# A fold of two weight matrices: w3 turned by VectorE in 32x32 squares instead of transposed on TensorE

## The chip, the cores and the metric

One core of one Trainium2 chip runs the whole program. The metric is device microseconds (us) of one execution, and the time of a kernel is the median of its runs.

## The reference

`x` is (8, 3904, 192) in float32, 31232 tokens in all. A causal convolution of seven taps comes first, whose weights are a softmax over the taps and are shared by the 24 channels of each of eight heads. Then comes a multiplicative network with two products of 192 to 1024, a square matrix of 1024x1024 and a projection back to 192:

```python
w = np.exp(weight - np.max(weight, axis=-1, keepdims=True))
w = w / (np.sum(w, axis=-1, keepdims=True) + 1e-09)
y[b, s, h, g] = sum_k w[h, k] * x_pad[b, s + k, h, g]      # causal, 7 taps
a = y @ w1                     # 192 -> 1024
b = y @ w2                     # 192 -> 1024
out = ((a * b) @ w3) @ w_out   # 1024 -> 1024 -> 192
```

## The kernel before

Nothing stands between the last two products, so the kernel computes W = w3 @ w_out (1024x192) once and uses W for all tokens. This is the fold that the change is about.

**The main work.** The tokens are two streams (NS = 2) of 15616, taken in rounds R of 512 tokens of each stream. `first_product(R)` has eight units, one for each f0 (a block of 128 of the 1024 features). A unit is six matmuls into `pa`, six into `pb` (L379), the eviction of `pa` to `asb` by ScalarE (L386) and the product of `asb` with `pb` into `abT` by VectorE (L388). I write 1.3 for the unit f0 = 3 of round 1. `second_product(R, r)` multiplies `abT` by `W_sb` (L404). All PSUM tiles, whatever they hold, come from one pool of four tiles of two banks in rotation (tag `banks`, L69), so a tile can be written only when the one of four allocations earlier has been read.

**The opening.** Rounds 0, 1 and 2 run `first_product` with other work between the units, put there by a dictionary from f0 to functions: the convolution of later batches of `x` (`conv`, L260, 32 matmuls of 32x32 for a half of the heads of one window parity), TensorE transposes of the first convolved batches (`pe_transposes`), and the fold. The four second products of rounds 0 and 1 come after round 2, and they are the first that need `W_sb`. After that the kernel goes in phases of two rounds.

**The fold.** `fold(j0)` runs at 1.3, 1.6, 2.1, 2.4 and 2.7. Each first runs `w3_product(j0 - 2)`, then `w3_transpose(j0)`. `w3_transpose` makes 16 TensorE transposes of 128x128 blocks of w3 (L449) into a PSUM tile `w3ps`, and VectorE copies that to `w3T` (L452). `w3_product` makes 16 matmuls of `w3T` with `wo_b` (L459) into `wps`, and ScalarE evicts it to `W_sb` (L464; in two halves at L462 for the last pair, j0 = 6, where both halves share the one tile `wps`).

**The loads.** GpSimd issues the loads of `x` (L117), of w_out (L438, one DMA) and of w3 (L442, eight DMAs of 128 rows) in program order, and the DMAs cast from float32 to bf16. Batch 3 of `x`, called x3 below, is four DMAs between the fourth and the fifth DMA of w3. Its first two are all that the first parity of its convolution reads. Each DMA issue takes one of eight semaphores in rotation and so waits until the DMA of eight issues earlier has landed. SyncE issues the stores of the convolved rows (L315), the DMA transposes that bring them back as `xT` for rounds 3 and later (L349), and the output.

Of the kernel before, what the change touches and what calls it, by code (L numbers as in the profile page):

```python
# [8 lines left out]
FP32 = mybir.dt.float32  # L9
BF16 = mybir.dt.bfloat16  # L10
# [6 lines left out]
def kernel(  # L17
# [10 lines left out]
    nc = tc.nc  # L28

    B, S, D = x.shape  # L30
    H, K = weight.shape
    G = D // H
    DFF = moe_w1.shape[1]
    JT = DFF // 128
# [10 lines left out]
    C = 32  # L45
# [15 lines left out]
    const = ctx.enter_context(tc.tile_pool(name="const", bufs=1))  # L61
    stage = ctx.enter_context(tc.tile_pool(name="stage", bufs=2))
# [5 lines left out]
    def banks(name):  # L68
        return psum.tile([128, NS, CH], FP32, tag="banks", name=name)  # L69

    def banks_bf16(name):
        return psum.tile([128, 16, 128], BF16, tag="banks", name=name)
# [18 lines left out]
    def group(r, e):  # L91
        return slice((2 * r + e) * C, (2 * r + e) * C + C)
# [13 lines left out]
    def load_x(b, parts=(0, 1)):  # L106
        tiles = xb_of.setdefault(b, {})
        zeros_of = zero_rows.setdefault(b, [])
        n, m, E = shape_of(b)
        for js in [v for q, v in enumerate(parts_of(b)) if q in parts]:  # L110
            xb = work.tile([128, len(js) * m, D], BF16, tag="xb", bufs=6, name="xb")
            for j in js:
                tiles[j] = (xb, (j - js[0]) * m)
            for e in range(E):
                for s, t, w in runs_of(b, js, e):
                    for r in range(NS):
                        nc.gpsimd.dma_start(  # L117
                            out=xb[group(r, e), s:s + w, :],
                            in_=bass.AP(tensor=x.tensor, offset=(r * TS + t - PAD) * D,
                                        ap=[[D, C], [E * ST * D, w], [1, D]]))  # L120
                for j in js:
                    for u in range(m):
                        i, s = FIRST[b] + j * n + u * E + e, tiles[j][1] + u
                        if i % WB == 0 and i:
                            zeros_of += [(xb, group(r, e).start, s) for r in range(NS)]
                        if i == NWIN - 1:
                            nc.gpsimd.memset(xb[group(1, e), s, :], 0.0)
                            t = tok(i) - PAD
                            nc.gpsimd.dma_start(out=xb[group(0, e), s, :],
                                                in_=x_rows[t:t + C, :])  # L130
                            p = group(1, e).start
                            nc.gpsimd.dma_start(out=xb[p:p + PAD + LAST, s, :],
                                                in_=x_rows[TS + t:TS + t + PAD + LAST, :])
# [6 lines left out]
    for r, queue in enumerate((nc.sync, nc.scalar)):  # L140
        p = group(r, 0).start
        queue.dma_start(out=begin[p:p + C, 1:HW, :], in_=bass.AP(
            tensor=x.tensor, offset=(r * TS + ST - PAD) * D,
            ap=[[D, C], [ST * D, HW - 1], [1, D]]))
# [5 lines left out]
        out=diag, in_=diag, pattern=[[-1, 128 + 8]], compare_op=ALU.is_equal,  # L150
        fill=0.0, base=0, channel_multiplier=1)
    ident = diag[:, 0:128]
# [13 lines left out]
    for i in range(4):  # L166
        d = diag[i * C:i * C + C, i * C + 2 * i:i * C + 2 * i + C]
        nc.vector.tensor_copy(
            out=cmask[i * C:i * C + C],
            in_=bass.AP(tensor=d.tensor, offset=d.offset, ap=[d.ap[0], [1, 2], [1, C]]))  # L170
# [11 lines left out]
    V, A, P = nc.vector.tensor_copy, nc.scalar.copy, nc.gpsimd.tensor_copy  # L182
# [10 lines left out]
    def warm(n, wd=CH):  # L193
# [13 lines left out]
        out=share[:, :, 0:K], in0=taps.unsqueeze(1).to_broadcast([H, H, K]), scalar=total,  # L207
# [7 lines left out]
    for i in range(4):  # L215
        ps = slice(i * C, i * C + C)
        nc.vector.tensor_copy(out=every[ps],
                              in_=diag[ps, ps].unsqueeze(1).to_broadcast([C, 4, C]))
    wsb = const.tile([128, H, 2, 2], BF16)
    nc.vector.tensor_copy(  # L220
        out=wsb, in_=spread[:, 0, 0:2 * H].rearrange("p (h k) -> p h k", h=H)
# [5 lines left out]
        out=cprod.rearrange("p h k (s two) -> p h k s two", two=2),  # L227
# [8 lines left out]
    for k in range(2):  # L236
# [3 lines left out]
            start=(k == 0), stop=(k == 1))  # L240
    nc.vector.tensor_copy(out=Aband,
                          in_=bps[:, 0, 0:C * H].rearrange("p (h s) -> p h s", s=C))
# [186 lines left out]


    W_sb = const.tile([128, JT, D], BF16)
    wo_b = const.tile([128, JT, D], BF16)
    w3r = moe_w3.rearrange("(jt jp) g -> jp jt g", jp=128)
    wor = moe_w_out.rearrange("(gt gp) d -> gp gt d", gp=128)
    w3b_of, w3T_of = {}, {}

    def load_wo():
        nc.gpsimd.dma_start(out=wo_b, in_=wor)  # L438

    def load_w3(jt):  # L440
        w3b_of[jt] = stage.tile([128, DFF], BF16, tag="w3b", bufs=JT, name="w3b")
        nc.gpsimd.dma_start(out=w3b_of[jt], in_=w3r[:, jt, :])  # L442

    def w3_transpose(j0):
        tps = banks_bf16("w3ps")
        for q in range(2):
            w3b = w3b_of.pop(j0 + q)
            for gt in range(JT):
                nc.tensor.transpose(out=tps[:, q * JT + gt, :],  # L449
                                    in_=w3b[:, gt * 128:(gt + 1) * 128], identity=ident)  # L450
        w3T_of[j0] = stage.tile([128, 2, JT, 128], BF16, tag="w3T", bufs=2, name="w3T")
        nc.vector.tensor_copy(out=w3T_of[j0].rearrange("p q g c -> p (q g) c"), in_=tps)  # L452

    def w3_product(j0):
        w3T = w3T_of.pop(j0)
        wps = banks("wps")
        for q in range(2):
            for gt in range(JT):
                nc.tensor.matmul(wps[:, q, 0:D], w3T[:, q, gt, :], wo_b[:, gt, :],  # L459
                                 start=(gt == 0), stop=(gt == JT - 1))  # L460
            if j0 + 2 == JT:
                nc.scalar.copy(out=W_sb[:, j0 + q, :], in_=wps[:, q, 0:D])  # L462
        if j0 + 2 < JT:
            nc.scalar.copy(out=W_sb[:, j0:j0 + 2, :], in_=wps[:, :, 0:D])  # L464


# [10 lines left out]
    for lo in (HC, HC + 256):  # L477
        for k in (0, 2, 1):
            swap_w(k, lo, lo + 256, (P, P))
    load_wo()  # L480
    for jt in range(4):
        load_w3(jt)

    def seq(*fs):
        def run():
            for f, *a in fs:
                f(*a)
        return run

    def fold(jt):  # L490
        if jt > 0:
            w3_product(jt - 2)
        if jt < JT:
            w3_transpose(jt)

    def later_loads():
        load_x(3)
        for jt in range(4, JT):
            load_w3(jt)
        for b in (4, 5, 6):  # L500
            load_x(b)

    first_product(0, {
        2: later_loads,
        4: seq((conv, 1, 0, 4)),
        5: seq((conv, 1, 4, 4)),
# [2 lines left out]
    first_product(1, {  # L509
        0: seq((conv, 2, 4, 4)),  # L510
        2: seq((pe_transposes, 2), (store, 2, LAG_ROWS // ST)),
        3: seq((fold, 0)),
        6: seq((fold, 2)),
        7: seq((conv, 3, 0, 4, (A,), (0,)))})
    first_product(2, {
        0: seq((conv, 3, 0, 4, (A,), (1,))),
        1: seq((fold, 4)),
        3: seq((conv, 3, 4, 4, (A,), (0,))),
        4: seq((fold, 6)),
        5: seq((conv, 3, 4, 4, (A,), (1,)), (store, 3), (transposes, 3), (transposes, 4)),  # L520
        7: seq((fold, 8))})
    sent[0] = 5


# [17 lines left out]
    for p, rounds in enumerate(phases):  # L542
# [9 lines left out]
        last = NR if p == len(phases) - 1 else done + 2  # L552
# [42 lines left out]
```

## Time and profile before

| What | Value |
|---|---|
| median of 3 runs | 527.5 us (527.0 to 527.67) |
| the profiled execution | 527.51 us, its span 525.8 us |
| PE, DVE, ACT, POOL busy | 519.0, 343.6, 333.7, 68.4 us |
| granted clock of TensorE | 1.0 |
| L449, 64 transposes of w3 | 4.2 us busy, 219 ns each |
| L459, 64 matmuls of the fold | 6.1 us busy, 246 ns each |
| L452, 4 copies of w3T | 4.9 us busy, 1223 ns each |
| L442, 8 DMA issues of w3 | 4.3 us busy on POOL, median 9.3 us to landing |
| L438, 1 DMA issue of w_out | 0.9 us busy on POOL, 5.4 us to landing |

The busy time of PE is the union of overlapping matmuls, and each one's listed duration is longer than the distance to the next one. The chain of waits gives the distances. PEld is the weight load ahead of each matmul, which overlaps the matmul before it.

### The profile page before, as it was taken

The numbers are of one execution on the slowest core, as the hardware profiler recorded it, in microseconds if no ns is written. First come the engines' busy times: TensorE is split into PE (matmuls) and PEld (weight loads), VectorE is DVE, ScalarE is ACT, GpSimd is POOL, SyncE is SP. The second block draws the span as 40 slices with busy tenths as digits, with TensorE's granted clock in tenths as the row PEclk, the third lists the DMA queues.
The fourth block names the chain that finished last, engine by engine and source line by source line (L and its number), as shares of the span: only waits on it lengthen the run. The fifth ranks groups of instructions, "written<-read, shape, count | busy, mean of one in ns | idle before, by whom it ended". The sixth has DMA issues, their size and how long they took to land.

```text
span 525.8 us, 14828 instructions
## 1 busy us (share of the span) xinstructions
PE 519.0 (99%) x6464; PEld 339.4 (65%) x6464; DVE 343.6 (65%) x327; ACT 333.7 (63%) x381; POOL 68.4 (13%) x129
## 2 busy tenths in 40 slices
PE   8999999999999999999999999999999999999997
PEld 4465774856748466484765847658575584856777
DVE  6786459478493874939659296692956829468380
ACT  4867467576574856747667475675747647466462
POOL 7846002004020010301002020020000000000000
PEclk9999999999999999999999999999999999999999
DMA  8999969956696475993779546795317543140304
GB/s 118 157 200 188 176 139 174 140 149 85 152 167 143 91 106 125 138 177 91 106 150 173 126 90 101 150 163 122 65 53 145 108 127 92 61 106 2 121 1 151
DMA packets 135351, 64.83 MB, mean 123 GB/s; under 512 B 87808, under 2 KB 134262, under 8 KB 135286
## 3 DMA queue, kind: packets, MB, share of 16 engines
q1 hardware_dynamic: 92495, 45.78, 40.3%
q0 software_dynamic: 42560, 17.97, 29.4%
q8 instruction: 50, 0.82, 0.6%
q10 hardware_dynamic: 231, 0.14, 0.1%
q14 instruction: 15, 0.12, 0.1%
HBM read 36.22 MB, written 34.80 MB: 135 GB/s over the span
## 4 chain that ended last, share of the span: by engine, by line
PE 95%; DVE 2%; ACT 1%; issue 1%; DMA 0%; DVEq 0%; ACTq 0%
PE ops L404 31%; PE pa L379 29%; PE pb L379 29%; PE cps L276 3%; DVE abT L388 1%; PE wps L459 1%; ACT asb L386 1%; PE w3ps L449 1%; DMA begin<-in_x_dram 0%; PE tps L324 0%; PE warm L196 0%; DVE ws L180 0%; ACT convo L284 0%; PE ops L422 0%; PE tps L339 0%
## 5 line engine op out<-in xcount | busy, mean ns | idle before, releaser
L388 DVE TENSOR_TENSOR abT<-asb,pb 128x1024 bf16<-128x1024 bf16 x240 | 293.0, 1221 | 85.0 <-ACT asb L386 68.2
L386 ACT CAST asb<-pa 128x1024 bf16<-128x1024 f32 x244 | 247.2, 1013 | 66.8 <-PE pa L379 66.8
L379 PE MATMUL pb<-xT,wn 64*128 64x512 bf16 (+1 forms) x744 | 198.5, 373 | 0.2 <-DVE abT L388 0.2
L379 PE MATMUL pa<-xT,wn 64*128 64x512 bf16 (+1 forms) x744 | 197.5, 373 | 0.2
L379 PE MATMUL pa<-xT,ws 64*128 64x512 bf16 (+1 forms) x744 | 197.6, 373 | 0.0
L379 PE MATMUL pb<-xT,ws 64*128 64x512 bf16 (+1 forms) x744 | 195.8, 373 | 0.0
L379 PEld LDWEIGHTS <-wn 64*128 64x128 bf16 x1488 | 137.9, 94 | 84.4 <-issue 2.2
L379 PEld LDWEIGHTS <-ws 64*128 64x128 bf16 x1488 | 131.1, 94 | 71.2 <-issue 1.6
L404 PE MATMUL ops<-W_sb,abT 128*128 128x192 bf16 x1936 | 166.8, 246 | 0.0
L404 PEld LDWEIGHTS <-abT 128*128 128x128 bf16 x1936 | 157.7, 98 | 9.3 <-issue 9.0
L409 ACT COPY osb<-ops 128x768 f32<-128x768 f32 (+1 forms) x61 | 48.4, 794 | 109.6 <-PE ops L404 109.6
L284 DVE CAST convo<-cps 128x320 bf16<-128x320 f32 (+4 forms) x44 | 31.6, 749 | 76.5 <-PE cps L276 75.0
L117 POOL DMA_DIRECT2D xb<-in_x_dram x74 | 48.4, 660 | 12.8 <-DMA xb<-in_x_dram 4.9
L284 ACT CAST convo<-cps 128x640 bf16<-128x640 f32 (+4 forms) x60 | 34.7, 624 | 3.3 <-PE cps L276 3.0
L550 POOL COPY pace<-abT 1x2 bf16<-1x2 bf16 x9 | 1.6, 176 | 250.3 <-DVE abT L388 250.3
L276 PE MATMUL cps<-xb,Aband 32*32 32x240 bf16 (+2 forms) x1344 | 17.0, 242 | 0.0
L276 PEld LDWEIGHTS <-Aband 32*32 32x32 bf16 x1344 | 9.9, 89 | 8.2 <-issue 6.6
L426 DVE COPY osb<-ops 128x192 f32<-128x192 f32 x1 | 0.4, 358 | 11.7 <-PE ops L422 11.7
L196 PE MATMUL warm<-zeros 128*128 128x512 bf16 (+1 forms) x13 | 5.7, 578 | 1.5 <-DVE one_rows L162 1.5
L459 PEld LDWEIGHTS <-w3T 128*128 128x128 bf16 x64 | 5.2, 98 | 2.4 <-issue 2.4
L459 PE MATMUL wps<-wo_b,w3T 128*128 128x192 bf16 x64 | 6.1, 246 | 0.6 <-ACT W_sb L462 0.4
L452 DVE COPY w3T<-w3ps 128x2048 bf16<-128x2048 bf16 x4 | 4.9, 1223 | 1.9 <-PE w3ps L449 1.9
(59 smaller groups left out, 61.6 us busy)
## 6 DMA issues: line engine op xcount, KB each, us to landing
out_dram<-osb SPq DMA_DIRECT2D x60, 384.0 KB
xb<-in_x_dram POOLq DMA_DIRECT2D x44, 240.0 KB, 6.9
rows<-convo SPq DMA_DIRECT2D x18, 240.0 KB
rows<-convo SPq DMA_DIRECT2D x18, 150.0 KB
w3b<-in_moe_w_dram POOLq DMA_DIRECT2D x8, 256.0 KB, 9.3
xT<-rows SPq DMA_TRANSPOSE x84
rows<-convo SPq DMA_DIRECT2D x11, 120.0 KB
xb<-in_x_dram POOLq DMA_DIRECT2D x4, 228.0 KB, 4.2
```

What stands on the lines that cost most here:

```text
L117: nc.gpsimd.dma_start(out=xb[group(r, e), s:s + w, :], in_=bass.AP(tensor=x.tensor, offset=(r * TS + t - PAD) * D, ap=[[D, C], [E * ST * D ...
L196: nc.tensor.matmul(t[:, j % 2, 0:wd], zeros[:, 0:128], zeros[:, 0:wd], start=True, stop=True)
L276: nc.tensor.matmul(o.rearrange("p (w g) -> p w g", g=wd)[:, :, q * G:(q + 1) * G], Aband[group(r, e), h0 + q, :], xb[group(r, e), s:s + m, ...
L284: f(out=convo[:, e::E, k, :, c0:c0 + c] .rearrange("p w r g -> p r w g"), in_=src[:, :, :, o:o + c])
L379: nc.tensor.matmul(p[:, r, f * N:f * N + N], w_of(i, k, r)[rs, ft * 128:(ft + 1) * 128], xT[k][rs, r0:r0 + N], start=(k == 0), stop=(k == ...
L386: nc.scalar.copy(out=asb[:, :, 0:per * N], in_=pa[:, :, 0:per * N])
L388: nc.vector.tensor_tensor(out=ab[:, f0, :, 0:N], in0=asb[:, :, 0:N], in1=pb[:, :, 0:N], op=ALU.mult)
L404: nc.tensor.matmul(ops[:, g // 2, (g % 2) * D:(g % 2) * D + D], ab[:, jt, r, g * 128:(g + 1) * 128], W_sb[:, jt, :], start=(jt == 0), stop ...
L409: nc.scalar.copy(out=osb.rearrange("p (a g) d -> p a (g d)", g=2), in_=ops[:, 0:ng // 2, 0:2 * D])
L449: nc.tensor.transpose(out=tps[:, q * JT + gt, :], in_=w3b[:, gt * 128:(gt + 1) * 128], identity=ident)
L452: nc.vector.tensor_copy(out=w3T_of[j0].rearrange("p q g c -> p (q g) c"), in_=tps)
L459: nc.tensor.matmul(wps[:, q, 0:D], w3T[:, q, gt, :], wo_b[:, gt, :], start=(gt == 0), stop=(gt == JT - 1))
```

## The change

The contraction of W = w3 @ w_out runs over the 1024 columns g of w3. The change splits g among partitions in another way: partition 32 i + a holds, for group gg (0 to 3) and t (0 or 1), column 256 i + 64 gg + 2 a + t. `wo_b` is loaded in that order, in four DMAs. A tile of w3 keeps 32 rows on each quarter of the partitions, with quarter i holding columns 256 i to 256 i + 255. Then one VectorE instruction for a pair of row blocks turns every 32x32 square of 4-byte pairs (two bf16 at a time), and the result has columns on the partitions. The matmuls read their weights from it with a step of two bf16, since t is innermost. The number and shapes of the product's matmuls stay as they were.

Besides this, w3 comes in three groups of four DMAs (4, 2 and 2 row blocks), the places of the product, the turn and the four convolutions of batch 3 between the units are new, and the last pair's halves get a PSUM tile each.

```diff
     def load_wo():
-        nc.gpsimd.dma_start(out=wo_b, in_=wor)
-    def load_w3(jt):
-        w3b_of[jt] = stage.tile([128, DFF], BF16, tag="w3b", bufs=JT, name="w3b")
-        nc.gpsimd.dma_start(out=w3b_of[jt], in_=w3r[:, jt, :])
-    def w3_transpose(j0):
-        tps = banks_bf16("w3ps")
-        for q in range(2):
-            w3b = w3b_of.pop(j0 + q)
-            for gt in range(JT):
-                nc.tensor.transpose(out=tps[:, q * JT + gt, :],
-                                    in_=w3b[:, gt * 128:(gt + 1) * 128], identity=ident)
-        w3T_of[j0] = stage.tile([128, 2, JT, 128], BF16, tag="w3T", bufs=2, name="w3T")
-        nc.vector.tensor_copy(out=w3T_of[j0].rearrange("p q g c -> p (q g) c"), in_=tps)
+        for i in range(4):
+            nc.gpsimd.dma_start(
+                out=wo_b[C * i:C * i + C].rearrange("a g t d -> a g (t d)"),
+                in_=bass.AP(tensor=moe_w_out.tensor, offset=i * GQ * D,
+                            ap=[[2 * D, C], [64 * D, GQ // 64], [1, 2 * D]]))
+    def load_w3(j0, n):
+        t = stage.tile([128, 4 * n, GQ], BF16, tag=f"w3b{j0}", bufs=1, name="w3b")
+        for j in range(j0, j0 + n, 2):
+            w3b_of[j] = (t, 4 * (j - j0))
+        for i in range(4):
+            nc.gpsimd.dma_start(
+                out=t[C * i:C * i + C],
+                in_=bass.AP(tensor=moe_w3.tensor, offset=j0 * 128 * DFF + i * GQ,
+                            ap=[[DFF, C], [C * DFF, 4 * n], [1, GQ]]))
+    def w3_turn(j0):
+        t, o = w3b_of.pop(j0)
+        w3T = stage.tile([128, GQ // 64, 2, 4, C, 2], BF16, tag="w3T", bufs=2, name="w3T")
+        nc.vector.transpose(
+            out=w3T.rearrange("p g q j b t -> p g (q j) (b t)").bitcast(FP32),
+            in_=t[:, o:o + 8, :].rearrange("p j (g c) -> p g j c", c=64).bitcast(FP32))
+        w3T_of[j0] = w3T
...
     def w3_product(j0):
-        wps = banks("wps")
+        last = j0 + 2 == JT
         for q in range(2):
-            for gt in range(JT):
-                nc.tensor.matmul(wps[:, q, 0:D], w3T[:, q, gt, :], wo_b[:, gt, :],
+            if q == 0 or last:
+                wps = banks("wps")
+            for g in range(GQ // 64):
+                for t in range(2):
+                    nc.tensor.matmul(wps[:, q, 0:D], w3T[:, g, q, :, :, t].rearrange("p j b -> p (j b)"), wo_b[:, g, t, :],
...
     first_product(1, {
         0: seq((conv, 2, 4, 4)),
         2: seq((pe_transposes, 2), (store, 2, LAG_ROWS // ST)),
-        3: seq((fold, 0)),
-        6: seq((fold, 2)),
-        7: seq((conv, 3, 0, 4, (A,), (0,)))})
+        3: seq((w3_turn, 0), (conv, 3, 0, 4, (A,), (0,))),
+        5: seq((w3_product, 0), (w3_turn, 2)),
+        7: seq((conv, 3, 0, 4, (A,), (1,)))})
     first_product(2, {
-        0: seq((conv, 3, 0, 4, (A,), (1,))),
-        1: seq((fold, 4)),
-        3: seq((conv, 3, 4, 4, (A,), (0,))),
-        4: seq((fold, 6)),
+        0: seq((w3_product, 2), (w3_turn, 4)),
+        2: seq((conv, 3, 4, 4, (A,), (0,))),
+        4: seq((w3_product, 4), (w3_turn, 6)),
         5: seq((conv, 3, 4, 4, (A,), (1,)), (store, 3), (transposes, 3), (transposes, 4)),
-        7: seq((fold, 8))})
+        7: seq((w3_product, 6))})
```

The loads keep their order: w_out, w3 blocks 0 to 3, x3, w3 blocks 4 to 7, then the batches 4, 5 and 6 of `x`.

More of the change, by code (lines that the diff above doesn't have):

```diff
@@ L431 @@
     W_sb = const.tile([128, JT, D], BF16)
-    wo_b = const.tile([128, JT, D], BF16)
-    w3r = moe_w3.rearrange("(jt jp) g -> jp jt g", jp=128)
-    wor = moe_w_out.rearrange("(gt gp) d -> gp gt d", gp=128)
+    GQ = DFF // 4
+    wo_b = const.tile([128, GQ // 64, 2, D], BF16)
     w3b_of, w3T_of = {}, {}
     def load_wo():
-        nc.gpsimd.dma_start(out=wo_b, in_=wor)
-    def load_w3(jt):
-        w3b_of[jt] = stage.tile([128, DFF], BF16, tag="w3b", bufs=JT, name="w3b")
-        nc.gpsimd.dma_start(out=w3b_of[jt], in_=w3r[:, jt, :])
@@ L454, in w3_product @@
     def w3_product(j0):
         w3T = w3T_of.pop(j0)
-        wps = banks("wps")
+        last = j0 + 2 == JT
         for q in range(2):
-            for gt in range(JT):
-                nc.tensor.matmul(wps[:, q, 0:D], w3T[:, q, gt, :], wo_b[:, gt, :],
-                                 start=(gt == 0), stop=(gt == JT - 1))
-            if j0 + 2 == JT:
+            if q == 0 or last:
[3 more added lines that the diff above has]
+                    nc.tensor.matmul(wps[:, q, 0:D], w3T[:, g, q, :, :, t].rearrange("p j b -> p (j b)"), wo_b[:, g, t, :],
+                                     start=(g + t == 0), stop=(g == GQ // 64 - 1 and t == 1))
+            if last:
@@ L462, in w3_product @@
                 nc.scalar.copy(out=W_sb[:, j0 + q, :], in_=wps[:, q, 0:D])
-        if j0 + 2 < JT:
+        if not last:
             nc.scalar.copy(out=W_sb[:, j0:j0 + 2, :], in_=wps[:, :, 0:D])
@@ L480 @@
     load_wo()
-    for jt in range(4):
-        load_w3(jt)
+    load_w3(0, 4)
     def seq(*fs):
@@ L488, in seq @@
         return run
[L490 to L494, printed above, removed]
     def later_loads():
         load_x(3)
-        for jt in range(4, JT):
-            load_w3(jt)
+        load_w3(4, 2)
+        load_w3(6, 2)
         for b in (4, 5, 6):
```

## The prediction

> **What bounds the kernel now.** I read the page first (busy time, then the chain that ended last), then the chain in order of time through the opening, the groups by shape, and the timelines of VectorE and GpSimd.
>
> ```profile
> PE 519.0 (99%) x6464; PEld 339.4 (65%) x6464; DVE 343.6 (65%) x327; ACT 333.7 (63%) x381; POOL 68.4 (13%) x129
> ...
> PE 95%; DVE 2%; ACT 1%; issue 1%; DMA 0%; DVEq 0%; ACTq 0%
> ```
>
> TensorE sets the time: what it is spared on that chain comes off the end, unless a wait takes its place. The fold's share, from the chain in order of time (start, us, what):
>
> ```profile
> 31.44 1.00 PE w3ps L449 x16
> ...
> 33.84 0.65 PE pa L379 x6
> ...
> 36.43 1.43 PE wps L459 x16
> 37.85 0.89 PE w3ps L449 x16
> 38.75 0.75 PE pa L379 x6
> ...
> 57.70 0.78 PE wps L459 x8
> 58.48 0.02 issue
> 58.50 0.33 ACT W_sb L462
> 58.83 0.04 issue
> 58.87 0.82 PE wps L459 x8
> ```
>
> Each of the four groups of transposes stands on the chain (the other two at 45.32 and 52.22, 0.89 each). A group that is not pa or pb costs about 0.1 on entry (1.00 against 0.89) and 0.1 on the pa behind it (0.75 against 0.65). In the last pair the second half waits for ScalarE's eviction, since both halves share a PSUM tile. The groups by shape (busy us, mean ns | idle before):
>
> ```profile
> L388 DVE TENSOR_TENSOR abT<-asb,pb 128x1024 bf16<-128x1024 bf16 x240 | 293.0, 1221 | 85.0 <-ACT asb L386 68.2 <-PE cps L276 1.5
> L452 DVE COPY w3T<-w3ps 128x2048 bf16<-128x2048 bf16 x4 | 4.9, 1223 | 1.9 <-PE w3ps L449 1.9
> L459 PEld LDWEIGHTS <-w3T 128*128 128x128 bf16 x64 | 5.2, 98 | 2.4 <-issue 2.4
> ```
>
> A unit costs PE 0.65 + 0.65 = 1.30, ScalarE 1.01 and VectorE 1.22 plus 0.03 between two. VectorE has only 0.05 to spare in a unit; it catches up only while PE does other work.
>
> **The change part by part. Transposes.** Sixteen take 0.89, so 55.6 ns each, and 64 take 3.56. In 1.3 to 2.7 there were nine groups of other work (transposes alone, three products with transposes, the last product, four convolutions). Now there are eight, four products and four convolutions: one entry and one exit less, 0.20. The last pair's halves get a tile each, and the wait of 0.41 (58.48 to 58.87 and 0.82 against 0.78) goes. What is late next is the second half's eviction (it starts 0.2 after the half's last matmul and takes 0.32), but only the eighth matmul of L404 needs it, 0.6 after the first. Together 4.17.
>
> **The turn.** Four copies of 1.22 become four transposes of 1024 four-byte elements per partition. No trace row shows this operation. Nearest is L388, 1024 results per partition in 1.22. The float32 cast from SBUF that fills `xb` from `begin` (1152 per partition in 0.75) would give 0.69 including its start, and two steps per element would give 2 x 1.07 + 0.15 = 2.29, with 0.15 the start that the casts of 320 and 640 (0.486 and 0.819) leave. I take 1.22. [...]
>
> The copies had 1 us of PE work of the same group to cover them, and the turns have none: behind a turn stands the next abT, and behind that the PSUM tile which PE needs four allocations later. I walked the new order by these durations. The same walk over the old order gives 59.50 for the start of L404, where the trace has 59.53. VectorE ends abT of 1.3 at 33.09, then come turn, abT, abT, turn, abT: the tile of pb at 1.6 is free at 36.84 + 2T, for T = 1.22 at 39.28. PE reaches unit 2.0 at 38.95 and waits 0.4. Another wait of 0.15, as before at 49.33, comes behind a convolution at 2.3. The second pair of turns is hidden, since each has a product of 1.34 beside it. Against the waits that the old order had (0.17 at 43.84, 0.15 at 49.33, 0.1 at 1.5), the extra is 0.2.
>
> **The strided weights.** The 64 weight loads now read every second bf16. In the trace a packed load hides under a transpose of 55.6 ns, and the product's matmuls are 86 apart (2.75 for 32 of the same shape in L404), so a load has 30 ns to grow. If it doubles to 111, the spacing becomes 111 and the four products lose 64 x 25 = 1.6. It may also cost nothing. I take nothing, because the listed 98 ns of a load overlaps the work before it in every group. [...]
>
> **The loads.** They come one after the other, as GpSimd's timeline shows:
>
> ```profile
> 17.95 0.90 POOL L438 DMA_DIRECT2D wo_b<-in_moe_w_out_dram  x1
> 18.83 2.17 POOL L442 DMA_DIRECT2D w3b<-in_moe_w_dram  x4
> 20.95 2.10 POOL L117 DMA_DIRECT2D xb<-in_x_dram  x3
> ...
> 30.57 0.70 POOL L117 DMA_DIRECT2D xb<-in_x_dram  x1 [0.76 <-DMA xb<-in_x_dram]
> 31.92 0.69 POOL L117 DMA_DIRECT2D xb<-in_x_dram  x1 [0.64 <-DMA xb<-in_x_dram]
> ```
>
> The last two rows are issues that waited for the first and second DMA of x3, which had landed just before. The first convolution of batch 3 stood at 40.08; now PE reaches it at 31.36, and its second matmul needs the second of these DMAs, at about 31.6. Ahead of it are now four DMAs of w_out with 128 pieces each (0.55 to issue, as for a w3 DMA of 128 pieces, against 0.90 for the single one, so data flows 0.35 earlier), and four DMAs of w3 with 512 pieces of 512 written bytes. A w3 DMA of 128 pieces of 2048 bytes lands every 1.25, an x DMA of 640 pieces of 384 bytes every 1.3: 156 and 32.5 ns per piece and DMA engine. Between them 512 bytes cost 42, so 32 pieces per engine take 1.34, four DMAs 0.4 more. If instead a piece costs as much per byte as in x, 43, it is the same; if the small pieces pay 55, it is 7.0 against 5.0. Hence the second x3 DMA lands between 31.6 - 0.35 + 0.4 = 31.65 and 33.3. I take 31.9, near the x rows: PE waits 0.54, but then comes to unit 2.0 later and the 0.4 there nearly goes, so 0.27 net. The turns wait for w3: the first at 33.1 for blocks that land about 29 (4 us spare), the third at 42 for blocks at about 37. The eight DMAs of w3 blocks 4 to 7 make the rest of GpSimd's queue (batches 4 to 6, the memsets of their zero rows at 51.6) some 0.7 later, and the first user of batch 4 is at 62.3, now 58.6. SyncE's queue keeps its order. Its store of batch 3 and the DMA transposes for round 3 (six issues from 61.52 in 9.93, the first three by 66.5) move up with the convolution. Round 3 moves from 72.54 to 68.8. If the loads of batches 5 and 6 held these transfers where they were, the third would land at 68 to 69: nothing to 0.5.
>
> **The sum.** 4.17 - 0.20 - 0.27 = 3.70. The profiled execution took 527.51, the median's 527.5: 523.8. Beyond 60 us PE's chain has no wait that hangs on absolute time, so the gain lasts.
>
> **Rivals.**
> - *The stride shows.* The load doubles: 2.1 instead of 3.7, so 525.4. For it: the loads' 98 ns are close to the 86 between matmuls. Against: transposes run at 55.6 with a load each.
> - *x3 is late.* At 33.6 PE waits 2.2 at 1.3, the gain is 2.0, 525.5; at 35 it is 0.6, 526.9. For it: the data flowed without a gap from 20 us. Against: it needs 57 ns for a piece of 512 bytes, where the x rows give 43.
> - *VectorE at half rate.* T = 2.29: the waits are 2T - 2.1 in the first pair of turns and about 2T - 3.0 in the second, 4.1 in all, 3.9 more than before; gain 0.3, 527.2, no measurable change.
> - *VectorE becomes the bound.* If every square of 32 pays a start of its own (the smallest VectorE row, a memset of one element, takes 59 ns; 32 squares per partition, 1.9), T = 3.1, the waits are 4.1 + 3.2, less 0.2, 7.1 in all: 2.9 slower, 530.4. It decides from T = 2.4, where the gain is gone; above it each 0.1 costs 0.4.
>
> That the transposes stay is ruled out: the built program has 64 fewer on PE and four transposes on VectorE.
>
> **How the numbers follow.** The measurement can tell about 0.2%, 1.05 us. Chances: forecast (gain 3.0 to 4.5) 0.62, stride 0.12, x3 late 0.11, half rate 0.08, VectorE bound 0.07. The last two, and x3 at 35, are beyond the range's upper end: 526.4 holds x3 to 34.5 and the stride with an x3 at 33. The lower end is 523.0: a turn of 0.69 and x3 in time give 4.2, and 0.3 is for distances rounded in the chain. Faster: 0.62 + 0.12 + 0.09 = 0.83. Same: the rest of x3 and half rate, 0.09. Slower 0.08.
>
> **What would show it.** Right: L449 and L452 gone, the turn near 1.2, 16 matmuls of the product in 1.4, a PE wait at 1.3 below 0.6 for x3, L404 starting near 55.8, the last W_sb without the 0.41. Wrong: a turn above 2, product matmuls over 100 apart, PE's wait at 1.3 above 2 us, or a gap ahead of round 3.

## The result, and the profile after

The changed kernel takes 526.28 us (median of 22 runs, 524.68 to 527.61), the kernel before 527.59 us in the same series. The ratio is 0.9977, 95% interval 0.9968 to 0.9987. It is faster by 1.3 us, where 3.7 were forecast. That the time still lies inside the predicted range is owed to the room left there for a late x3, and not to the forecast. The profiled execution took 525.07 us with a span of 523.4.

The page of the changed kernel: busy time by engine, and the shares of the chain that ended last.

```profile
PE 515.3 (98%) x6399; PEld 335.0 (64%) x6400; DVE 343.4 (66%) x327; ACT 333.7 (64%) x381; POOL 72.3 (14%) x136
...
PE 92%; POOL 3%; DMA 3%; DVE 1%; ACT 0%; issue 0%; DVEq 0%; POOLq 0%
```

PE is spared 3.7 us of busy time, as removing the transposes should do. But GpSimd and DMA, which had nothing or 0% of the chain before, now have 3% each: the chain goes back through the loads. The groups by shape (busy us, mean ns | idle before):

```profile
L469 PE MATMUL wps<-wo_b,w3T 128*128 128x192 bf16 x64 | 6.0, 247 | 0.0
L469 PEld LDWEIGHTS <-w3T 128*128 128x128 bf16 x64 | 5.1, 98 | 1.7 <-issue 1.7
L456 DVE STREAM_TRANSPOSE w3T<-w3b 128x1024 f32<-128x1024 f32 x4 | 5.0, 1238 | 0.0
```

The turn takes 1.24 us and the strided weight loads keep their 98 ns. The chain in order of time (start, us, what):

```profile
22.59 0.66 POOL xb L117
23.25 9.73 DMA xb<-in_x_dram
32.99 0.04 issue
33.03 0.40 PE cps L276 x31
33.43 0.76 PE pa L379 x6
...
36.13 1.43 PE wps L469 x16
...
55.46 1.43 PE wps L469 x16
56.89 2.64 PE ops L404 x32
```

The two rows at 22.59 and 23.25 are the new thing: in this opening PE no longer follows its own work but waits for the second DMA of x3. From the waits of PE and the timeline of GpSimd:

```profile
PE cps L276 <- DMA xb<-in_x_dram: 1.1, 1, 1.1
```

```profile
17.88 2.16 POOL L438 DMA_DIRECT2D wo_b<-in_moe_w_out_dram  x4
20.04 2.56 POOL L448 DMA_DIRECT2D w3b<-in_moe_w_dram  x4
22.59 2.74 POOL L117 DMA_DIRECT2D xb<-in_x_dram  x4
```

L404 starts at 56.89, against 59.70 before: 2.81 earlier. Here is its row in the chain before, and the start of the transposes of batch 2 in the timelines, before and after:

```profile
59.70 2.64 PE ops L404 x32
```

```profile
29.02 1.01 PE L324 MATMUL tps<-diag,convo 128*128 128x128 bf16 x15
29.40 1.01 PE L324 MATMUL tps<-diag,convo 128*128 128x128 bf16 x15
```

The opening of this execution happened to be 0.38 late, so from there on 3.19 us were won. At the end of these two executions 2.44 are left.

### The profile page after: what moved, and what is told of

It reads as the page before. It is cut to its first block, busy times and chain, and to the rows that moved or that the text cites. A ratio compares the mean times of both kernels' runs of the same rounds, so it can differ in the third digit from the quotient of the medians.

```text
span 523.4 us, 14709 instructions
## 1 busy us (share of the span) xinstructions
PE 515.3 (98%) x6399; PEld 335.0 (64%) x6400; DVE 343.4 (66%) x327; ACT 333.7 (64%) x381; POOL 72.3 (14%) x136
## 4 chain that ended last, share of the span: by engine, by line
PE 92%; POOL 3%; DMA 3%; DVE 1%; ACT 0%; issue 0%; DVEq 0%; POOLq 0%
PE ops L404 31%; PE pa L379 29%; PE pb L379 28%; PE cps L276 2%; DMA xb<-in_x_dram 2%; PE wps L469 1%; POOL ws L180 1%; POOL xb L117 1%; DMA wn<-in_moe_w_dram 1%; POOL w3b L448 0%; DVE abT L388 0%; POOL wo_b L438 0%; ACT asb L386 0%; PE ops L422 0%; POOL wn L186 0%
## 5 line engine op out<-in xcount | busy, mean ns | idle before, releaser
L388 DVE TENSOR_TENSOR abT<-asb,pb 128x1024 bf16<-128x1024 bf16 x240 | 292.8, 1221 | 84.8 <-ACT asb L386 67.9
L404 PE MATMUL ops<-W_sb,abT 128*128 128x192 bf16 x1936 | 167.0, 246 | 0.1
L404 PEld LDWEIGHTS <-abT 128*128 128x128 bf16 x1936 | 157.6, 98 | 9.6 <-issue 9.3
L284 DVE CAST convo<-cps 128x320 bf16<-128x320 f32 (+4 forms) x44 | 31.6, 750 | 76.4 <-PE cps L276 76.4
L448 POOL DMA_DIRECT2D w3b<-in_moe_w_dram x12 | 7.2, 600 | 6.4 <-DMA w3b<-in_moe_w_dram 3.4
```

What stands on the lines that cost most here:

```text
L284: f(out=convo[:, e::E, k, :, c0:c0 + c] .rearrange("p w r g -> p r w g"), in_=src[:, :, :, o:o + c])
L388: nc.vector.tensor_tensor(out=ab[:, f0, :, 0:N], in0=asb[:, :, 0:N], in1=pb[:, :, 0:N], op=ALU.mult)
L404: nc.tensor.matmul(ops[:, g // 2, (g % 2) * D:(g % 2) * D + D], ab[:, jt, r, g * 128:(g + 1) * 128], W_sb[:, jt, :], start=(jt == 0), stop ...
L448: nc.gpsimd.dma_start(out=t[C * i:C * i + C], in_=bass.AP(tensor=moe_w3.tensor, offset=j0 * 128 * DFF + i * GQ, ap=[[DFF, C], [C * DFF, 4 ...
```

## The experiments

The theory: the exchange of transposes for turns is worth what was forecast, and what is missing goes to a late x3, which the new form of the loads delays, and to what its stop sets off. The rivals: the turns or the strided weights cost more than their rows show, or the gain is lost further on, behind the first L404. Unless another is named, the base is the changed kernel, and ratios are to the kernel before, run on the same chip (527.8 to 528.1 us).

**The changed kernel once more.**

> The changed kernel once more, unchanged, as the control of this group and for a second profile. Theory W (the missing gain is the wait of the first convolution of batch 3, at unit 1.3, for the second DMA of x3): that DMA lands at about 33 again, and where an execution is slower than 525.1 it lands later still; median about 526.3. Theory E (the missing gain is lost elsewhere, for instance in the first 20 us or after 60 us): the wait at 1.3 is as in the first profile, 1.1 to 1.5, whatever the execution's time.

Measured: 525.96 us (525.27 to 527.2), 0.9969 (0.9956 to 0.9982). The profiled execution was the longest of the seven, 527.2. Its waits, its chain, and its windows (from and to, length, busy us of PE, PEld, DVE, ACT and POOL with counts, granted clock, DMA share, GB/s):

```profile
PE cps L276 <- DMA xb<-in_x_dram: 2.7, 2, 1.6
```

```profile
33.97 0.59 PE cps L276 x23
34.57 1.40 PE pa L379 x6
35.96 1.28 PE pb L379 x6
...
59.31 2.64 PE ops L404 x32
```

```profile
32.00:34.00 2.00, 0.25 (x9) 0.12 (x10) 1.91 (x2) 0.00 (x0) 0.91 (x2) 0.93 1.59 190
34.00:36.00 2.00, 2.00 (x39) 0.89 (x40) 0.00 (x0) 1.02 (x2) 1.08 (x2) 0.50 1.54 194
36.00:38.00 2.00, 2.00 (x16) 0.78 (x14) 0.65 (x1) 1.07 (x2) 0.48 (x2) 0.71 1.45 192
```

Here x3's second DMA landed at 33.93, not 32.99, and PE stood still for 1.6 and 1.0 us. Then the granted clock fell to half of full speed. A unit's six matmuls took 1.40 and 1.28 in place of 0.76 and 0.65. From the windows, the half clock lasted 0.07 x 2 / 0.5 + 2.0 + 0.29 x 2 / 0.5 = 3.44 us (the trace's own record of the clock has 3.41), which costs half of it, 1.7. L404 starts only 0.39 earlier than before.

The 22 runs of the changed kernel fall into two groups by the mean granted clock. Ten had 0.999 or 1.0, and their median is 525.3. Twelve had 0.994 to 0.997, and theirs is 527.1; one drop of 3.41 us lowers the mean by 0.003. Not every lowered mean comes from this place: the profiles with x3 first, with the later convolution, with only w3 old and with batch 6 behind the second convolution show the half clock at 8 to 12 us, in the opening (0.50 or 0.51 in the window from 8 to 10), and took 524.36 to 525.27. Of 44 executions of the kernel before that ran beside the experiments, 11 had a mean of 0.997, and their median is 527.8 like that of the others, so there a drop cost nothing that can be seen. How many of the twelve had one at 1.3 is therefore not known. Eleven of them took 526.4 or more.

**x3 first, and x3 last.** Batch 3 is loaded ahead of w_out and w3 (w3 then in four groups of two row blocks), or behind all of w3.

```diff
 # x3 first
+    load_x(3)
     load_wo()
-    load_w3(0, 4)
+    load_w3(0, 2)
+    load_w3(2, 2)
 ...
-        load_x(3)
 # x3 last
     def later_loads():
-        load_x(3)
         load_w3(4, 2)
         load_w3(6, 2)
+        load_x(3)
```

> The loads of x3 go ahead of w_out and w3, and w3 comes in four groups of two row blocks so that the first turn still has its blocks in time. Theory W: no wait at 1.3 (x3 lands near 27), the first turn not late, L404 starts near 55.5 to 55.9 and the time is 1.2 below the changed kernel if only the wait of its first profile is typical, and up to 2.5 below it (523.8) if x3 lands later than that in most executions; the spread of the runs shrinks. Theory E: the wait goes but the time stays within 0.5 of the changed kernel.

> The loads of x3 go behind all eight row blocks of w3, so x3 lands later by the time of four row blocks, some 5.4: at about 38.3. Theory W: the wait at 1.3 grows from 1.3 to 6.7 and the time rises by about 5.3 over the changed kernel, to 531.5. Theory E: TensorE's wait is absorbed by slack that the later units leave, and the time rises by under 2.

x3 first: 524.65 us (12 runs, ten of them 524.3 to 525.2, two at 527.3 and 529.4), 0.9956 (0.9938 to 0.9973). The chain:

```profile
31.27 0.33 PE cps L276 x32
...
55.21 2.64 PE ops L404 x32
...
64.65 0.24 PE cps L276 x28
64.89 1.19 issue
66.08 0.49 PE cps L276 x36
```

Without the wait at 1.3, L404 starts 4.49 earlier than before, so the late x3 is where that part of the gain went. But 1.2 us are lost again at 64.89, in the third convolution after the first L404, with no data wait there. For the two long executions there is no profile.

x3 last: 533.49 us, 1.0112 (1.0097 to 1.0128). PE waits 6.8 us for x3, and the time is 2 us above what that wait alone had let me expect:

```profile
38.87 0.59 PE cps L276 x27
39.47 1.39 PE pa L379 x6
40.86 1.28 PE pb L379 x6
42.14 1.28 PE pa L379 x6
```

At full clock these four take 0.33, 0.76, 0.65 and 0.65, so they are 2.15 us longer: the half clock again (0.50 in the windows from 34 to 42 us), and about the missing amount.

**The convolution later.** The first convolution of batch 3 is moved from 1.3 to 1.6.

```diff
-        3: seq((w3_turn, 0), (conv, 3, 0, 4, (A,), (0,))),
+        3: seq((w3_turn, 0)),
         5: seq((w3_product, 0), (w3_turn, 2)),
+        6: seq((conv, 3, 0, 4, (A,), (0,))),
```

> The loads stay as in the changed kernel, but the first convolution of batch 3 runs after unit 1.6 instead of 1.3, at about 37, when x3 has landed. Theory W: no wait for x3; two convolutions in a row load ScalarE, which costs 0.35 by the walk, so 0.9 below the changed kernel if its first profile is typical, up to 2 below it if not. Theory E: within 0.5 of the changed kernel or above it.

Measured: 525.23 us (524.82 to 526.03), 0.9954 (0.9941 to 0.9967). No wait for x3 and no half clock at this place, but PE now waits 0.3 once for a turn. L404 starts at 55.76, 3.94 earlier than before, and a stop of 1.5 us follows at 65.44, again in the third convolution.

**The old forms of the loads.** First both, then each alone. The instructions on PE and VectorE are those of the changed kernel. The values of w_out or w3 then land in other places than the product needs, so these kernels tell of times only.

```diff
 # w_out (both, and w_out alone)
-        for i in range(4):
-            nc.gpsimd.dma_start(out=wo_b[C * i:C * i + C]..., in_=bass.AP(...))
+        nc.gpsimd.dma_start(out=wo_b.rearrange("p g t d -> p (g t) d"),
+                            in_=moe_w_out.rearrange("(gt gp) d -> gp gt d", gp=128))
 # w3 (both, and w3 alone)
-        for i in range(4):
-            nc.gpsimd.dma_start(out=t[C * i:C * i + C], in_=bass.AP(...))
+        for j in range(n):
+            nc.gpsimd.dma_start(out=t[:, 4 * j:4 * j + 4, :].rearrange("p j g -> p (j g)"),
+                                in_=moe_w3[(j0 + j) * 128:(j0 + j) * 128 + 128, :])
```

> The changed kernel with the loads of before in shape: w_out in one DMA, w3 in eight DMAs of 128 partitions with 4 KB rows, in the same places of the queue. The values of w_out and w3 land in the wrong places, so the output is not the reference's; every instruction after the loads is the changed kernel's. Theory S (the new shape of the w_out and w3 loads holds back x3: between 20.5 and 27.5 us the DMA engines moved 50 to 85 KB per half us, where they moved 90 to 110 before): the second x3 DMA lands at 31.6 as in the kernel before, the wait at 1.3 is under 0.5, no half clock, and the time is 524.3 to 525.0. Rival (x3 is late for another reason, such as GpSimd's issue order or HBM): x3 lands at 33 or later again and the time is about 526.

> Edit: the changed kernel with w_out loaded by the single DMA of before (128 partitions, pieces of 384 bytes), w3 loaded as in the changed kernel; w_out's values land in other places, so the output is not the reference's. Which of the two loads costs the 2.1 us between the changed kernel (526.1) and the one with both old forms (524.0)? Theory S1 (w_out's four DMAs of 32 partitions, whose third and fourth land 2.7 us after the first two): the second DMA of x3 lands about 32.0 to 32.5, PE waits below 1.1 at 1.3, median 524.0 to 524.7. Theory S2 (w3's pieces of 512 bytes): it lands at 32.9 to 33.9 as in the changed kernel, 525.7 to 526.3. Both in part: 525.0.

> Edit: the changed kernel with w3 loaded by eight DMAs of 128 rows as before (pieces of 2048 bytes), w_out loaded as in the changed kernel; w3's values land in other places, so the output is not the reference's. Theory S1 (w_out's four DMAs cost the 2.1): x3's second DMA still lands at 32.9 or later, median 525.5 to 526.3. Theory S2 (w3's pieces of 512 bytes cost them): x3's second DMA lands by 32.5, wait at 1.3 below 1.1, median 524.0 to 524.7. Both in part: 525.0.

Both old: 524.02 us (523.39 to 524.3), 0.9922 (0.991 to 0.9935). That is 3.76 below the kernel before, the forecast amount. The timeline of PE shows what is left of the wait at 1.3: the convolution takes 0.77 instead of 0.40.

```profile
32.14 0.77 PE L276 MATMUL cps<-xb,Aband 32*32 32x120 bf16 x32
```

Only w_out old: 524.75 us (524.34 to 525.86), 0.9939 (0.9926 to 0.9951). Only w3 old: 524.27 us (523.88 to 524.79), 0.9925 (0.9912 to 0.9939). Either one alone brings most of the 2.1 back, so neither S1 nor S2 holds as written, nor do the parts add up in the median. The single profiles tell more. From GpSimd's first w_out issue to the landing of x3's second DMA:

| Kernel | first w_out issue | landing | between |
|---|---|---|---|
| before | 17.95 | 31.6 | 13.7 |
| both loads old | 18.61 | 32.47 | 13.9 |
| only w_out old | 17.86 | 32.44 | 14.6 |
| only w3 old | 17.99 | 32.99 | 15.0 |
| changed, first profile | 17.88 | 32.99 | 15.1 |
| changed, once more | 18.50 | 33.93 | 15.4 |

By these executions, one of each, w_out's four small DMAs cost 1.1 and w3's new form (small pieces, each DMA for 32 partitions) 0.7, each beside the other's old form. Beside the other's new form it is only 0.5 to 0.8 and 0.1 to 0.4, and both together cost 1.2 to 1.5. The rate in three windows (last column GB/s), of the kernel before, the changed one, and the one with only w3 old:

```profile
22.00:24.00 2.00, 2.00 (x46) 1.00 (x50) 1.86 (x3) 1.37 (x3) 1.47 (x3) 1.00 1.31 219
24.00:26.00 2.00, 2.00 (x77) 0.91 (x61) 1.25 (x2) 1.96 (x4) 0.83 (x2) 1.00 1.07 199
26.00:28.00 2.00, 1.95 (x24) 1.24 (x18) 1.22 (x1) 2.00 (x4) 0.55 (x1) 1.00 1.21 200
```

```profile
22.00:24.00 2.00, 2.00 (x27) 1.23 (x26) 1.49 (x3) 1.38 (x3) 1.95 (x4) 1.00 1.22 147
24.00:26.00 2.00, 2.00 (x48) 0.77 (x45) 1.63 (x3) 1.96 (x4) 1.85 (x3) 1.00 1.09 126
26.00:28.00 2.00, 1.83 (x47) 0.85 (x46) 1.22 (x1) 2.00 (x4) 0.39 (x2) 1.00 1.20 149
```

```profile
22.00:24.00 2.00, 1.98 (x25) 1.32 (x26) 1.37 (x2) 1.38 (x3) 2.00 (x4) 1.00 0.96 140
24.00:26.00 2.00, 2.00 (x48) 0.74 (x44) 1.67 (x3) 1.96 (x4) 1.02 (x2) 1.00 0.97 136
26.00:28.00 2.00, 1.93 (x46) 0.88 (x45) 1.24 (x2) 2.00 (x4) 0.59 (x2) 1.00 1.04 185
```

Before, 199 to 219 GB/s flow. With the new w_out ahead, the rate is 126 to 149 until 28 us, and it stays at 136 to 140 until 26 us even when w3 comes in its old pieces of 2048 bytes. So the low rate doesn't need small pieces of w3. They have a part of their own, though: with only w_out old, the same three windows have 162 to 180. What holds the flow down is not settled. The DMA engines were not full (the column before the last: 1.0 to 1.3 busy of each 2 us, before and after), and the same w_out DMAs and the first small pieces of w3, loaded behind x3 in the run with x3 first, flowed at 196 and 197 GB/s from 26 to 30 us.

The execution with only w_out old tells more of when the clock falls:

```profile
PE cps L276 <- DMA xb<-in_x_dram: 1.8, 2, 1.0
```

```profile
32.00:34.00 2.00, 1.52 (x39) 0.73 (x40) 1.29 (x2) 1.01 (x2) 0.65 (x3) 0.75 1.58 191
34.00:36.00 2.00, 2.00 (x12) 0.69 (x10) 0.48 (x1) 1.02 (x2) 1.14 (x2) 0.50 1.45 194
36.00:38.00 2.00, 2.00 (x20) 1.16 (x17) 1.03 (x2) 1.01 (x1) 1.86 (x3) 0.89 1.45 193
```

PE came early (at 30.48) and waited 0.77, ran one matmul, and waited 1.02. After a sum of 1.8 the clock fell to half for 3.44 us by the windows; this execution took 525.86, the longest of its five. Single waits of 0.96 (only w3 old) and 1.07 (changed, first profile) left it at 1.00, and so did the stops of 1.19 (x3 first) and 1.52 (the later convolution) behind L404. The trace's record of the granted clock adds something: its changes in this execution lie 27.31, 3.41 and 488.11 us apart, which are 8, 1 and 143 times 3.413, and the other profiles show whole multiples too: the stretch at full clock is 515.41 in the first profile of the kernel before and 512.00 in that of the changed one, 151 and 150 times. In the 3.41 us that ended with the fall, PE had stood still for 1.8 us here, 2.4 in the changed kernel once more, 2.2 with x3 last and 2.1 with batch 6 in round 3. Where a stretch counted off in this way held 0.96, 1.07 or 1.19, the clock stayed. With the later convolution the fall in the opening (7.8 us by the windows) puts a border at 65.9, inside the stop, so at most 1.1 of its 1.52 lie in one stretch. My estimate from these eight profiles is that the idle time inside one stretch counts, with the limit between 1.2 and 1.8; no run tested it. If so, a small shift of the landing decides over 1.7 us, and that fits either load alone bringing most of the median back. It isn't shown for each of the runs, since each kernel has one or two profiles.

**Filling the wait.** Eight matmuls that nothing uses, 1.83 us, ahead of the convolution at 1.3.

```diff
-        3: seq((w3_turn, 0), (conv, 3, 0, 4, (A,), (0,))),
+        3: seq((w3_turn, 0), (warm, 8), (conv, 3, 0, 4, (A,), (0,))),
```

> The changed kernel with eight useless matmuls of 512 columns on TensorE, 1.7 us, between unit 1.3 and the first convolution of batch 3, so that TensorE is not idle while it waits for x3. Theory C (a wait of 1.6 costs twice, because the granted clock falls to half behind it, and a wait of 1.1 does not): the clock stays at 1.0, the executions near 527 go and the median is 525.2 to 525.6, 0.6 below the changed kernel in spite of more work. Rival (the clock is not set by this wait): the useless work is added where x3 is in time, and the median is 526.3 or more with half-clock slices still there.

Measured: 526.36 us (525.34 to 526.88), 0.997 (0.9958 to 0.9982). Four of five executions had a mean clock of 1.0, and the profiled one kept 1.00 throughout with no wait for x3. But the filler is longer than the wait of 1.07 it replaces, and the median is no better than the changed kernel's, so the time that theory C named did not come. The clock agrees with theory C, and the time doesn't prove it.

**Batch 6 later.** Base: x3 first. Among its DMA queues the page of the changed kernel has this one:

```profile
q8 instruction: 50, 0.82 MB, 0.6%
```

That is 50 packets of 16 KB. PE has 12799 records (6399 matmuls and 6400 weight loads), 256 to a packet; before it had 12928, also with 50 packets. Theory F says that the stop in the third convolution is PE waiting for such a packet, which is late because of the loads. From 60 to 66 us of the run with x3 first, the DMA engines were busy 1.41, 1.68 and 1.26 of each 2 us, so they were not full. First batch 6 waits for round 3, then for the second convolution after L404 (about 62.5 us).

```diff
-        for b in (4, 5, 6):
+        for b in (4, 5):
             load_x(b)
 # in round 3
+            if p == 1 and j == 0:
+                P(out=pace, in_=abT_of[R][0:1, 2, 1, 0:2])
+                load_x(6)
 # or, behind the second convolution
+            if p == 0 and n == 1:
+                P(out=pace, in_=convo_of[4][0:1, 0, NP - 1, 0, 0:2])
+                load_x(6)
```

> The kernel with x3 loaded first, and the loads of batch 6 moved from the opening to round 3 (about 74 us; they are used from 96). Theory F (with x3 in time, 1.2 us of the gain is lost again at the third convolution after L404 starts, where TensorE stops after 28 of 64 matmuls with all data there, because the 16 KB fetch of its next instructions queues behind loads and stores that saturate the DMA engines up to 66 us): the fetch starts before 62, the stop of 1.2 is gone, and the time is 523.3 to 523.7. Rival (the stop belongs to this place in the program, or to a wait for data): the stop of 1.2 is still there and the time stays at 524.6.

> Edit: batch 3 loaded first, as in the run with x3 ahead of w_out and w3, and batch 6 loaded behind the second convolution of the first group of second products (from about 62.5 us) instead of behind batch 5 (46 to 53 us) or in round 3. Theory F (the 1.2 us stop in the third convolution is TensorE waiting for its own next 16 KB of instructions, which queue behind the loads of x): the loads of batches 4 and 5 are through by 60, the instructions arrive by about 62.5, no stop in the third convolution, the gain of about 4.4 at the first L404 is kept, and batch 6 lands by about 80 to 88, ahead of its first use at about 96: 523.2 (range 522.8 to 523.9), or 0.4 to 1.4 below the run with x3 first (524.65). Rival (the stop belongs to the convolution itself, or the loads of batch 6 at 62.5 meet the transfers of round 3): a stop of about 1.2 remains at 65 to 70, 524.6 or more.

In round 3: 525.78 us (524.37 to 528.12), 0.9971 (0.9956 to 0.9987). The stop is gone (that packet comes at 61.4, with x3 first at 63.4). But batch 6 lands at 98.3, PE waits 1.3 and 0.9 us for it, and the clock falls to half once more at 99: in the profiled execution, the longest of twelve, 4.3 us are lost in the second products behind round 4.

Behind the second convolution: 524.29 us (524.06 to 525.34), 0.9934 (0.9922 to 0.9946). The chain in the group of second products:

```profile
62.46 0.66 PE cps L276 x64
63.12 2.75 PE ops L404 x32
65.86 0.66 PE cps L276 x64
```

No stop: the third convolution takes 0.66 like the others, and the packet comes at 61.4 here too. Smaller stops without a data wait (0.23 at 95.91, 0.48 at 102.50) remain.

The place of the stops speaks for theory F as well. Behind the first 20 us, five profiles (the first of the changed kernel, x3 first, the later convolution, the filler and this one) have eight stops of PE that no data wait ends, from 0.08 to 1.52 us long. Count PE's records from the start, matmuls and weight loads together: the stops stand behind record 704 or 705, 1985, 2752 or 2753, and 3008. These are multiples of 256 apart, give or take one, also in the kernel with the filler, whose program is shifted by 16 records, and 256 is the number of records to a packet that the page gives. In all eight PE went on 1.3 to 1.8 us after the transfer of the last packet had ended. So by these counts and times the stops belong to the packets and not to the convolution. That the packets come late because of the loads rests on the two runs that moved batch 6.

The median is 0.4 below that of x3 first, with overlapping intervals, so this part is inconclusive. Against the changed kernel the intervals are apart: with the loads in their new form, this is the shortest time.

## Why the prediction was right and wrong

*Transposes, entries, the last pair (4.17).* Right. The four groups of w3ps are gone from the chain, L404 follows the last product at once (55.46 + 1.43 = 56.89), and without a wait for x3 the whole sum is there: with x3 first, L404 follows the transposes of batch 2 by 26.35 us, before by 30.68, which is 4.33. In the run with the later convolution it is 26.67, so 4.01, with 0.3 more of a wait for a turn.

*The turn (1.22).* Right, though the value was a choice among the nearest rows: 1.24, at 33.39, 37.77, 43.80 and 51.02. The rivals of 2.29 and 3.1 are out.

*PSUM waits (0.20).* This term did not come. The 0.4 that was forecast at unit 2.0 is about 0.15 (at 40.67, where a pa takes 0.82 in place of 0.65), and at 2.3 it is 0.15 as forecast (46.69). The old order had 0.17 and 0.15 at such places, so nothing extra was lost. With x3 first unit 2.0 has the same 0.82 (at 38.99), so the late x3 isn't what took the rest away.

*The stride (0).* Right: 16 matmuls in 1.43 with both layouts, 98 ns per load.

*The loads (0.27).* This is the step that failed. The text gave 31.65 to 33.3 for x3's second DMA and took 31.9, the end near the x rows. It was 32.99 and 33.93. The wrong term was "so data flows 0.35 earlier": the four w_out DMAs were counted by the time to issue them, and at the rate of a full queue from then on. In fact they cost 1.1 beside the old form of w3, and w3's new form cost 0.7 beside the old one of w_out, where 0.4 were estimated; both together cost 1.2 to 1.5. PE waited 1.07 in place of 0.54, and it had no longer wait at 2.0 to save in return, so the whole wait counts: 4.17 - 1.07 = 3.10, and the profile has 3.19 from the transposes of batch 2 to L404.

*The price of a late x3.* The rival was named, with 525.5 for 33.6. For 33.93 it would have been about 525.8, but that execution took 527.2. What no rival had is the clock: behind two stops of 1.6 and 1.0 us it was at half for 3.44 us, 1.7 us more. By the mean clocks that may have happened in up to half of the executions.

*"Beyond 60 us PE's chain has no wait that hangs on absolute time."* Wrong. Of the 2.81 at L404, 0.13 are lost in the third convolution and 0.26 at 94 to 97; with an earlier PE it was 1.2 and 1.5. The stop was ended by no semaphore that the profile shows, it stands multiples of 256 of PE's records from the other stops, and moving batch 6 out of the way took it away twice. Round 3 itself found its xT in time.

*Why the two profiles differ.* GpSimd's path to the loads and PE's path to 1.3 don't wait for each other. GpSimd's first w_out issue came at 17.86 to 18.61 over the executions, following a DMA of `wn` that took 3.73 to 4.53, and the transposes of batch 2 started at 28.06 to 30.12. Before, the first user of x3 came at 40.08, and this difference was of no account. The change made it decide.

So the forecast part (transposes for turns) is worth what was said, 3.76 with the old loads. What failed is the time at which x3 lands, and with it what a late x3 costs. In the first profile the bill closes: of the forecast 3.70, 0.5 are missing in the stretch of the fold, 0.4 went to the later opening of that execution and 0.4 to the stops behind L404, which leaves the 2.4 that it had. The median gained only 1.3. The second profile shows what a longer execution lost, a wait of 2.6 and 1.7 by the clock. How the two mix in the other executions, which have no profile, stays open.

## What to carry to other kernels

When a change reshapes loads, price the whole queue behind them, and where the traces give bounds 1.6 us apart for a landing, ask which end also costs a clock: here 1.7 us at once, behind waits of 1.8 us in all and of 2.65 alike. A use that is moved 9 us ahead deserves its load moved too: x3 loaded first and batch 6 later brought 524.29. The page has 50 instruction packets of 16 KB among the DMAs, and PE stopped for up to 1.52 us with all its data there, until 1.3 to 1.8 us after the latest of them had been transferred. Look at which loads run at that time.

## What the runs showed of the hardware that was not expected

- The granted clock of TensorE fell to 0.50 after waits of 0.77 and 1.02 with one matmul between, and not after single waits of 0.96 and 1.07 or a stop of 1.52. It stayed there for 3.41 us (in two profiles at 1.3, in one behind round 4), and for 10.2 us, three times that, around the wait of 6.8.
- A transpose of 1024 four-byte elements per partition in squares of 32 took VectorE 1.24 us, hardly more than the elementwise product of 1024 (L388, 1.22).
- Behind four DMAs of 128 pieces of 768 bytes, each for 32 partitions, the DMA engines moved 126 to 149 GB/s for some 6 us, where the old form had 199 to 219. With w3 in its old form behind them it was 136 to 140 for 4 us. Behind x3, in a filled queue, the same four moved at 196.
- All eight stops of PE without a data wait behind the first 20 us stand multiples of 256 of PE's records apart, give or take one, and PE went on 1.3 to 1.8 us after the last 16 KB packet of instructions had been transferred.
